# A gated mix of a long convolution and a shift MLP: permuted frequencies, re-homed scratch, and the gate on ScalarE

## The chip, the core and the metric

One core of a Trainium2 chip runs the whole kernel. The metric is device time in microseconds (us) for one execution; a run's time is that of the core from launch to end, and the comparisons use the median of several runs. The engines are TensorE (PE; PEld is its weight load), VectorE (DVE), ScalarE (ACT), GpSimd (POOL) and SyncE (SP), which here only issues DMAs.

## The reference

Two branches share the input x = q of shape (1, 2048, 640), in bf16, and a gate per row mixes them:

```python
x = A_q
g = _sigmoid((x * gate_w).sum(-1, keepdims=True))
a = _A_ref(x, A_k, A_v, A_shift_k, A_ssm_k, A_ssm_D)
b = _B_ref(x, B_w1, B_w2, B_w3, B_w4)
return g * a + (1 - g) * b
```

Branch A: a causal convolution of four taps over k gives k_shift, kv = k_shift * v, then a causal convolution of kv over all 2048 rows with a filter of 2048 taps per channel (`ssm_k`), computed with FFTs of 4096 points along the rows; a skip term kv * ssm_D is added and the result is multiplied by q.

Branch B: h = gelu(layernorm(x) @ w1); the four quarters of its columns are shifted by +1, -1, +2 and -2 rows and multiplied by w2 (x1 = x + hs); then x1 + gelu(layernorm(x1) @ w3) @ w4, with 1536 columns between w3 and w4.

## The kernel before, in words

**Tiles.** Row 16p + n of the sequence lies on partition p in tile n, so there are 16 tiles u = 0 to 15 of 128 x 640, in four groups of four. `Q` holds x and is overwritten with x1 and then with the MLP's result. The hidden rows lie transposed in `GS`, with the row shift made while they are written.

**The long convolution** is a two-step Fourier transform made of matmuls. `step1` multiplies a group of rows by the matrix F1 (128 x 128, cosine and sine part), ACT copies the result from PSUM to an `AR` tile, and ACT's queue stores it to a DRAM scratch tensor: `SH` for the filter (`filt`, 32 units over four groups), `SX` for kv (`signal`, 32 units). `spectrum` runs over 32 groups of frequencies t: `spec_h` reads SH back (BH), multiplies by M2[t] and copies to HS, two DMAs swap the halves of HS; `spec_x` does the same for SX (BX, XPB) and DVE multiplies the two spectra; `spec_z` multiplies by G1[t] and G2[t], copies to ZG (ACT and DVE in turn) and stores to `SZ`. `y_group` reads SZ (ZT), multiplies by F1T, applies the gate and q (`ty`) and adds the other branch.

**The matrices** M2, G1 and G2 are 128 x 4096 each and are made on the chip. POOL writes index patterns, DVE makes integer phases from them (the tile GEN), and ACT takes the sine. A matrix column belongs to one of four residues j, and only the partitions of the same residue may be nonzero: `gen_matrix` therefore runs four sines for each matrix, one for each j, with a scale and a bias for each partition that are zero on the others. Such a masked sine writes 1024 elements:

```python
for j in range(4):
    nc.scalar.activation(out=dst[:, :, :, :, j], in_=jv, func=ACT.Sin,
                         bias=mbias[:, j:j + 1], scale=mscale[:, j:j + 1])
```

**The filter** `A_ssm_k` is loaded as five tiles HN; `filter_transpose` transposes each on PE into the four tiles HT, with ACT and DVE copying from PSUM in turn.

**Branch B** is `norm_stats` and `norm_apply` (DVE statistics, the power for 1/sqrt on POOL, DVE's xn, transposes on PE, DVE's copy to XNT), `first_product` (W1, gelu on ACT into GS), `second_product` (W2, added to Q by DVE), `third_product` (W3, gelu on ACT into G) and `fourth_product` (W4, added to Q by DVE, then scaled by 1 - g on ACT; for the last group on DVE, with the store).

**Gate.** `gate_dot` multiplies x by the gate's weights on POOL and sums on ACT, a tile at a time (scr); `gate_act` makes G32 (g) and OMG (1 - g).

**Short convolution.** `short_conv` needs the taps CJ, laid out from CJR by four POOL copies, the tiles KT and VT of the group, and three rows of the neighbouring partition (KHALO). DVE makes it in acc and tmp.

**Order.** The program is written for one scheduler that keeps, on each engine, the program's order as a priority: an instruction whose inputs and buffers are expected earlier may be put ahead, and the resulting order is fixed for each engine. Waits are for data and for buffers. `merge(a, b, ratio)` interleaves two generators by costs written by hand; a falls first, b gets ratio times its cost. The main sequence is: norms and products for groups 0 and 1 with the filter's transposes, the sine matrices, the gate's first half, then `merge(chain(second_product(US[0]), first_product(2, X2)), filt(), 0.5)`, group 3 and the gate's second half, then the mixer (`mixer_front`) merged with `signal`, then `spectrum` merged with the rest of the MLP, then the output.

**Buffers.** Tiles of one tag share a number of buffers: "b5" has 11 (HN, HT, CJR, CJ, KHALO, KT, VT, acc, tmp, AR, BH, BX, HS, ZG, ZT), "w" has 3 (W12, GEN, W3, W4, XPB), "xnt" 2 (XNT), "g" 3 (the gelu tiles G), "r" 6 (xn, scr, ty, DROW), "gs" 1 (GS, later XQ, a second copy of q). In PSUM the tag "pc" has two (transforms and filter transposes) and "pm" two (the MLP).

Of the kernel before, what the change touches and what calls it, by code (L numbers as in the profile page):

```python
# [9 lines left out]
ACT = mybir.ActivationFunctionType  # L10
# [7 lines left out]
def kernel(  # L18
# [25 lines left out]
    nc = tc.nc  # L44
# [106 lines left out]
    pf4 = consts.tile([P, 1], F32, name="pf4")  # L151
    nc.vector.tensor_scalar(out=pf4[:], in0=pidx[:], scalar1=4.0, scalar2=1.0, op0=ALU.mult, op1=ALU.add)

    GEN = main.tile([P, 15, 256], F32, name="GEN", tag="w", bufs=3)

    def gen_i(a, n, dtype):
        return GEN[:, a:a + n, :].rearrange("p a b -> p (a b)").bitcast(dtype)

# [3 lines left out]
    for gi, (dst, col_mul, col_add, prow) in enumerate(((F1, 4, 1, pf), (F1T, 1, 0, pf4))):  # L162
        ic = gen_i(2 * gi, 1, I32)[:, 0:P]
        nc.gpsimd.iota(ic, pattern=[[col_mul, P]], base=col_add, channel_multiplier=0)
        jj = gen_i(2 * gi + 1, 1, I32).rearrange("p (c k) -> p c k", c=2)
# [9 lines left out]
    M2 = consts.tile([P, KH, 2, 16, 4], BF16, name="M2")  # L175
    G1 = consts.tile([P, KH, 2, 16, 4], BF16, name="G1")
    G2 = consts.tile([P, KH, 2, 16, 4], BF16, name="G2")
    midp = pbits(120, 0.125, 0, "midp")
    klo = pbits(3, 1, 0, "klo")
    basep = pbits(3, 16, 1, "basep")  # L180
    basei = pbits(60, 128, 0, "basei")
    nc.vector.tensor_tensor(out=basei[:], in0=basei[:], in1=basep[:], op=ALU.add)
    offp = [pbits(4, -512, 6144 + 2048 * ro, f"offp{ro}") for ro in range(2)]
    offi = [pbits(64, -64, 6144 - 2048 * o, f"offi{o}") for o in range(2)]
    mscale = consts.tile([P, 4], F32, name="mscale")
    mbias = consts.tile([P, 4], F32, name="mbias")
    for j in range(4):
        nc.vector.tensor_scalar(out=mscale[:, j:j + 1], in0=klo[:], scalar1=float(j), scalar2=2 * PI_ / TU,
                                op0=ALU.is_equal, op1=ALU.mult)
        nc.vector.tensor_scalar(out=mbias[:, j:j + 1], in0=klo[:], scalar1=float(j), scalar2=-PI_,  # L190
                                op0=ALU.is_equal, op1=ALU.mult)
    m0, m1 = gen_i(4, 2, F32), gen_i(6, 2, F32)

    def gen_phase():
        icf, ick, icn = gen_i(8, 2, I32), gen_i(10, 2, I32), gen_i(12, 2, I32)
        nc.gpsimd.iota(icf.rearrange("p (g i n) -> p g i n", i=4, n=16), pattern=[[64, 8], [4, 4], [512, 16]],
                       base=0, channel_multiplier=0)
        nc.gpsimd.iota(ick.rearrange("p (g i n) -> p g i n", i=4, n=16), pattern=[[64, 8], [4, 4], [0, 16]],
# [3 lines left out]
        nc.vector.tensor_scalar(out=m0, in0=icf, scalar1=basep[:], scalar2=midp[:], op0=ALU.add, op1=ALU.mult)  # L202
        nc.vector.scalar_tensor_tensor(out=m1, in0=ick, scalar=basei[:], in1=icn, op0=ALU.add, op1=ALU.mult)

    def gen_matrix(k):
        dst, src, offs = ((M2, m0, (offp[0][:], offp[1][:])), (G1, m1, (offi[0][:], offi[1][:])),
                          (G2, m1, (0.0, 6144.0)))[k]
        slot = (8, 0, 8)[k]
        jj = gen_i(slot, 4, I32)
        for o in range(2):  # L210
            nc.vector.tensor_scalar(out=jj[:, 512 * o:512 * o + 512], in0=src, scalar1=offs[o], scalar2=None,
                                    op0=ALU.add)
        nc.vector.tensor_scalar(out=jj, in0=jj, scalar1=TU - 1, scalar2=None, op0=ALU.bitwise_and)
        jv = jj.rearrange("p (o m n) -> p m o n", o=2, n=16)
        for j in range(4):
            nc.scalar.activation(out=dst[:, :, :, :, j], in_=jv, func=ACT.Sin,  # L216
                                 bias=mbias[:, j:j + 1], scale=mscale[:, j:j + 1])
# [4 lines left out]
    SZ = dram.tile([P, 32, D], BF16, name="SZ")  # L222
# [24 lines left out]
    def filter_transpose(dt):  # L247
        if not HT:
            HT.extend(big("HT") for _ in range(NG))
# [105 lines left out]
    KT, VT = [], []  # L355

    def load_cj():
        cjr = big("CJR", [P, D, 4])
        nc.gpsimd.dma_start(out=cjr[:], in_=A_shift_k.partition_broadcast(P))
        cj = big("CJ")  # L360
        for j in range(4):
# [346 lines left out]
```

## Time and profile before

| | us |
|---|---|
| median of 3 runs (lowest, highest) | 349.83 (349.45, 350.97) |
| profiled execution | 351.51 |
| its span, first to last instruction | 349.7 |
| PE busy | 260.7 |
| DVE busy | 205.3 |
| ACT busy | 193.3 |
| POOL busy | 57.9 |

The DMAs move 59.6 MB, at a mean of 170 GB/s over the span. The mean granted TensorE clock is 0.891 of full speed.

A group's line in the profile reads: source line, engine, operation, output tile <- input tiles, their shapes, count | busy us in all, mean ns of one | us that the engine was idle just before them, and what ended most of it. A line of waits reads: engine, tile and line that waited <- what ended the wait: us in all, times, longest. A windows line gives each engine's busy time and instructions in a stretch of the span, the granted clock, DMA's busy share and GB/s. Matmul durations overlap, so sums of busy time over a stretch are used rather than means. "SPq" and "ACTq" are the queues from which DMAs are issued.

### The profile page before, as it was taken

To read this page: it belongs to the slowest core of one execution; us is meant where nothing else is said; L and a number is where in the kernel's file an instruction comes from. 1 tells how busy PE (TensorE), PEld (TensorE's weight loads), DVE (VectorE), ACT (ScalarE), POOL (GpSimd) and SP (SyncE) were. 2 spreads that over 40 slices of the span, in tenths; PEclk is the share of its full clock that TensorE was granted. 3 is DMA by queue.
4 is the path that set the end of the run, shared out by engine and by line. 5 is a ranking of instruction groups with operands and counts; after the bars stand their busy time and mean duration, and the time that the engine had idled before them with its cause. 6 is when DMAs were issued, how large, how long until landed. Compare 5 with 4: busy or idle time off the path is not lost.

```text
span 349.7 us, 4290 instructions
## 1 busy us (share of the span) xinstructions
PE 260.7 (75%) x1572; PEld 154.7 (44%) x1572; DVE 205.3 (59%) x391; ACT 193.3 (55%) x271; POOL 57.9 (17%) x84
## 2 busy tenths in 40 slices
PE   2445967205683289999999999999999999742685
PEld 1433454002331246457754667446665556421343
DVE  4999956200006985549699993225664444541995
ACT  1123899998899102461456417968766788530000
POOL 4366873119004011100020010000000000000000
PEclk9999989755855559999999999999999999995989
DMA  8999200006669200006222286547897776738943
GB/s 281 245 330 378 81 1 2 0 12 220 219 194 379 103 2 0 3 28 199 75 75 78 75 320 255 147 191 216 237 287 259 221 244 186 225 114 306 366 154 112
DMA packets 32643, 59.59 MB, mean 170 GB/s; under 512 B 7375, under 2 KB 23887, under 8 KB 32622
## 3 DMA queue, kind: packets, MB, share of 16 engines
q1 hardware_dynamic: 19726, 42.77, 38.0%
q10 hardware_dynamic: 12672, 15.73, 12.7%
q0 software_dynamic: 224, 0.82, 0.7%
q8 instruction: 12, 0.20, 0.2%
q14 instruction: 9, 0.07, 0.1%
HBM read 35.71 MB, written 18.35 MB: 155 GB/s over the span
## 4 chain that ended last, share of the span: by engine, by line
PE 44%; DVE 19%; ACT 18%; DMA 11%; SPq 4%; issue 4%; POOL 0%; DVEq 0%; ACTq 0%; POOLq 0%
PE psw L431 11%; PE psw L418 10%; PE psw L321 5%; ACT G L216 5%; PE psz L494 4%; PE psw L404 4%; DMA BX<-SX 4%; DVE xn L279 3%; ACT AR L90 3%; ACT M L216 3%; SPq L124 3%; DVE acc L393 3%; PE ps L233 2%; DVE tmp L391 2%; PE psh L465 2%
## 5 line engine op out<-in xcount | busy, mean ns | idle before, releaser
L431 PE MATMUL psw<-W,G 128*128 128x320 bf16 x384 | 62.2, 303 | 0.1
L418 PE MATMUL psw<-XNT,W 128*128 128x512 bf16 x240 | 57.5, 379 | 0.6 <-DVE XNT L95 0.4
L90 ACT CAST AR<-ps 128x640 bf16<-128x640 f32 x64 | 41.1, 695 | 22.1 <-PE ps L233 22.1
L483 DVE TENSOR_TENSOR XPB<-XPB,HS 128x640 bf16<-128x640 bf16 x64 | 28.5, 487 | 41.1 <-ACT XPB L90 41.1
L431 PEld LDWEIGHTS <-G 128*128 128x128 bf16 x384 | 37.9, 99 | 16.0 <-issue 0.3
L233 PE MATMUL ps<-HT,F 128*128 128x320 bf16 x64 | 19.0, 409 | 22.6 <-ACT HT L90 15.9
L311 ACT ACTIVATE G<-psw 128x1024 bf16<-128x1024 f32 x24 | 24.7, 1029 | 18.6 <-PE psw L418 18.4
L418 PEld LDWEIGHTS <-W 128*128 128x128 bf16 x240 | 23.4, 98 | 24.8 <-issue 1.3
L286 PE MATMUL pst<-IDB,xn 128*128 128x128 bf16 x160 | 16.1, 274 | 23.5 <-DVE xn L279 19.6
L321 PE MATMUL psw<-XNT,W 128*128 128x512 bf16 x100 | 28.2, 439 | 4.9 <-DVE Q L407 2.4
L233 PEld LDWEIGHTS <-F 128*128 128x128 bf16 x128 | 13.6, 108 | 40.5 <-issue 33.9
L265 DVE BATCH_NORM_STATS2 st<-Q 128x6 f32<-128x320 bf16 x64 | 27.3, 466 | 4.1 <-DMA Q<-in_A_q_dram 4.0
L345 POOL TENSOR_TENSOR scr<-Q,GWB 128x640 bf16<-128x640 bf16 x16 | 22.9, 1461 | 36.7 <-ACT scr L346 35.7
L92 ACT ACTIVATE HS<-psh 128x640 bf16<-128x640 f32 x32 | 22.4, 708 | 11.1 <-PE psh L465 10.8
L90 ACT CAST XPB<-psx 128x640 bf16<-128x640 f32 x32 | 22.2, 693 | 6.4 <-PE psx L478 5.9
L494 PE MATMUL psz<-XPB,G 128*128 128x320 bf16 x128 | 22.7, 298 | 3.7 <-DVE ZG L95 1.2
L286 PEld LDWEIGHTS <-xn 128*128 128x128 bf16 x160 | 13.8, 126 | 26.1 <-DVE xn L279 21.2
L404 PE MATMUL psw<-W,GS 128*128 128x320 bf16 x160 | 23.1, 301 | 0.6 <-DVE XNT L95 0.6
L536 PE MATMUL psy<-ZT,F1T 128*128 128x320 bf16 x64 | 13.4, 344 | 13.5 <-DMA ZT<-SZ 8.7
L279 DVE TENSOR_SCALAR xn<-Q,mv,rs 128x640 bf16<-128x640 bf16 x32 | 19.0, 649 | 2.5 <-POOL rs L270 2.5
L539 DVE SCALAR_TENSOR_TENSOR ty<-psy,G,XQ 128x640 bf16<-128x640 f32 x16 | 13.5, 880 | 11.0 <-PE psy L536 11.0
L321 PEld LDWEIGHTS <-W 128*128 128x128 bf16 x100 | 11.1, 111 | 19.9 <-issue 11.4
(97 smaller groups left out, 369.8 us busy)
## 6 DMA issues: line engine op xcount, KB each, us to landing
SH<-AR ACTq DMA_DIRECT2D x8, 640.0 KB, 4.1
SX<-AR ACTq DMA_DIRECT2D x8, 640.0 KB, 3.3
BH<-SH SPq DMA_DIRECT2D x8, 640.0 KB, 4.3
HS<-HS SPq DMA_DIRECT2D x32, 160.0 KB, 3.1
BX<-SX SPq DMA_DIRECT2D x8, 640.0 KB, 4.8
SZ<-ZG ACTq DMA_DIRECT2D x8, 640.0 KB, 3.8
ZT<-SZ SPq DMA_DIRECT2D x8, 640.0 KB, 6.0
W<-in_B_w_dram SPq DMA_DIRECT2D x2, 1920.0 KB, 11.6
```

Of the source, the lines that this page charges most:

```text
L90: nc.scalar.copy(out=o, in_=i)
L216: nc.scalar.activation(out=dst[:, :, :, :, j], in_=jv, func=ACT.Sin, bias=mbias[:, j:j + 1], scale=mscale[:, j:j + 1])
L233: nc.tensor.matmul(ps[:, comp, 0:HD], lhsT=F1[:, comp, :], rhs=src[:, c0:c0 + HD], start=True, stop=True)
L265: nc.vector.bn_stats(out=st[:, h, :], in_=src[i][:, h * HD:(h + 1) * HD])
L279: nc.vector.tensor_scalar(out=xn[:], in0=src[i], scalar1=mv[:, i, 0:1], scalar2=rs[:, i:i + 1], op0=ALU.subtract, op1=ALU.mult)
L286: nc.tensor.transpose(out=pst[:, dd, i * P:(i + 1) * P], in_=xns[i][:, (d0 + dd) * P:(d0 + dd + 1) * P], identity=IDB[:])
L321: nc.tensor.matmul(ps[:, j, :], lhsT=W1P[:, dt, nt * P:(nt + 1) * P], rhs=XNT[:, dt, :], start=(dt == 0), stop=(dt == DT - 1))
L404: nc.tensor.matmul(ps[:, h, 0:HD], lhsT=GS[:, nt, u, :], rhs=W2P[:, nt, h * HD:(h + 1) * HD], start=(nt == 0), stop=(nt == DT - 1))
L418: nc.tensor.matmul(ps[:, j, :], lhsT=W3[:, dt, (f + j) * P:(f + j + 1) * P], rhs=XNT[:, dt, :], start=(dt == 0), stop=(dt == DT - 1))
L431: nc.tensor.matmul(ps[:, h, 0:HD], lhsT=G[ft // 4][:, ft % 4, i * P:(i + 1) * P], rhs=W4[:, ft, h * HD:(h + 1) * HD], start=(ft == 0), sto ...
L483: nc.vector.tensor_tensor(out=xp[:, 1 + a, :], in0=xp[:, 0, :], in1=HS[t // 2][:, a, t % 2, :], op=ALU.mult)
L494: nc.tensor.matmul(pz[:, h, 0:HD], lhsT=gm[:, t].rearrange("p a b c -> p (a b c)"), rhs=XP[t][:, 1 + a, h * HD:(h + 1) * HD], start=(a == ...
```

## The change

- **Layout of the matrices.** The frequencies are permuted so that in M2, G1 and G2 the residue j is no longer the innermost index: M2 is [128, 32, 2, 4, 16] and G1, G2 are [128, 32, 4, 2, 16]. A masked sine then writes runs of 16 (M2) or 32 (G1, G2) neighbouring elements. The inverse's index constants follow, with a mask of their own, and some more constants of one column are made.
- **SZ** is [4, 32, 32, 640]; a ZG tile is stored with one step over all 128 partitions. Each row is still a run of 1280 bytes, each ZT read four rows in a run.
- **Phases.** The 15 KB tile GEN in "w" gives way to three tiles of 4 KB in "g". `gen_phase` and the three `gen_matrix` become `gen_forward` (M2), placed ahead of the first norm, and `gen_inverse` (G1, G2), placed ahead of the first product.
- **HT.** Three of its four tiles become one tile HTA in "w"; the fourth, HTB, stays in "b5".
- **CJR** moves to "xnt", and `load_cj` to the start of the sequence. The halo and the first KT, VT are written ahead of the first product, the second KT, VT ahead of the filter's transform.
- **Sequence.** The filter's transform is merged with `second_product(US[0])` alone; X2's norm, `first_product(2)` and the statistics of group 3 come behind it, with the first two parts of `signal`'s short convolution between them. The gate's first half comes ahead of the filter's last transpose, its second half behind `first_product(2)`. `mixer_front` is merged with the rest of `signal` at 0.6.
- **Spectrum.** The four XQ loads stand within it, at t = 10, 14, 18 and 22. The last `third_product` is taken out of the merge, whose ratio becomes 0.75, and runs behind it.
- **End.** `ty` is made in two steps: ACT copies from PSUM with the scale g, DVE multiplies by XQ in bf16.

```diff
-    GEN = main.tile([P, 15, 256], F32, name="GEN", tag="w", bufs=3)
+    def gen_tile():
+        t = main.tile([P, 1024], I32, name="GEN", tag="g", bufs=3)
+        return t[:]
+
+    GA, GB, GC = gen_tile(), gen_tile(), gen_tile()
...
-    M2 = consts.tile([P, KH, 2, 16, 4], BF16, name="M2")
-    G1 = consts.tile([P, KH, 2, 16, 4], BF16, name="G1")
-    G2 = consts.tile([P, KH, 2, 16, 4], BF16, name="G2")
+    M2 = consts.tile([P, KH, 2, 4, 16], BF16, name="M2")
+    G1 = consts.tile([P, KH, 4, 2, 16], BF16, name="G1")
+    G2 = consts.tile([P, KH, 4, 2, 16], BF16, name="G2")
...
+    def masked_sines(dst, jj, ms, inner):
+        nc.vector.tensor_scalar(out=jj, in0=jj, scalar1=TU - 1, scalar2=None, op0=ALU.bitwise_and)
+        jv = jj.rearrange("p (o m n) -> p m o n", o=2, n=16)
+        for j in range(4):
+            nc.scalar.activation(out=dst[:, :, :, j, :] if inner else dst[:, :, j, :, :], in_=jv, func=ACT.Sin,
+                                 bias=ms[:, 1, j:j + 1], scale=ms[:, 0, j:j + 1])
+
+    def gen_forward():
+        icf = GA[:, 0:512]
         nc.gpsimd.iota(icf.rearrange("p (g i n) -> p g i n", i=4, n=16), pattern=[[64, 8], [4, 4], [512, 16]],
                        base=0, channel_multiplier=0)
+        for ro in range(2):
+            nc.vector.tensor_scalar(out=GC[:, 512 * ro:512 * ro + 512], in0=icf, scalar1=midp[:],
+                                    scalar2=offp[ro][:], op0=ALU.mult, op1=ALU.add)
+        masked_sines(M2, GC, masks[0], True)
+
+    def gen_inverse():
+        ick, icn, m1 = GA[:, 512:1024], GB[:, 0:512], GB[:, 512:1024].bitcast(F32)
...
         nc.vector.scalar_tensor_tensor(out=m1, in0=ick, scalar=basei[:], in1=icn, op0=ALU.add, op1=ALU.mult)
+        for (dst, jj, offs) in ((G1, GA, (offi[0][:], offi[1][:])), (G2, GC, (0.0, 6144.0))):
+            for o in range(2):
+                nc.vector.tensor_scalar(out=jj[:, 512 * o:512 * o + 512], in0=m1, scalar1=offs[o], scalar2=None,
+                                        op0=ALU.add)
+            masked_sines(dst, jj, masks[1], False)
...
-    SZ = dram.tile([P, 32, D], BF16, name="SZ")
+    SZ = dram.tile([4, 32, 32, D], BF16, name="SZ")
...
-            HT.extend(big("HT") for _ in range(NG))
+            hta = weights("HTA", [P, 3, 4, D])
+            HT.extend([hta[:, g] for g in range(3)] + [big("HTB")[:]])
...
-        cjr = big("CJR", [P, D, 4])
+        cjr = main.tile([P, D, 4], BF16, name="CJR", tag="xnt", bufs=2)
...
-                tensor=SZ.tensor, offset=SZ[16 * kg, 0, 0].offset,
-                ap=[[D, 32], [128 * D, 4], [32 * D, 4], [1, D]]), in_=zg[:])
+                tensor=SZ.tensor, offset=SZ[0, 4 * kg, 0, 0].offset,
+                ap=[[D, P], [1024 * D, 4], [1, D]]), in_=zg[:])
...
+            if t % 4 == 2 and 2 <= t // 4 < 6:
+                g = (3, 0, 1, 2)[t // 4 - 2]
+                nc.sync.dma_start(out=XQ[:, 4 * g:4 * g + 4, :], in_=qv[:, 4 * g:4 * g + 4, :])
...
-            nc.vector.scalar_tensor_tensor(out=halves(ty[:]), in0=ps[:, :, 0:HD], scalar=G32[:, u:u + 1],
-                                           in1=halves(XQ[:, u, :]), op0=ALU.mult, op1=ALU.mult)
+            evac("a", halves(ty[:]), ps[:, :, 0:HD], G32[:, u:u + 1])
+            nc.vector.tensor_tensor(out=ty[:], in0=ty[:], in1=XQ[:, u, :], op=ALU.mult)
...
+    CJ = load_cj()
+    gen_forward()
     st0 = norm_stats(tiles_of(c4[0]))
...
     filter_transpose(1)
-    gen_phase()
+    gen_inverse()
...
     load_q(3)
+    KHALO = load_halo()
+    load_kv(0)
     X1 = norm_apply(tiles_of(c4[1]), st1, "v")
     run(first_product(0, X0))
-    st2 = norm_stats(tiles_of(c4[2]))
     filter_transpose(2)
     filter_transpose(3)
     run(first_product(1, X1))
-    gen_matrix(0)
-    gen_matrix(1)
-    gen_matrix(2)
+    st2 = norm_stats(tiles_of(c4[2]))
     gate_dot(0)
-    X2 = norm_apply(tiles_of(c4[2]), st2, "v")
+    gate_dot(1)
     filter_transpose(4)
-    gate_dot(1)
-    KHALO = load_halo()
-    CJ = load_cj()
-    load_kv(0)
     W3 = weights("W3", [P, DT, Fh])
     nc.sync.dma_start(out=W3[:], in_=B_w3.rearrange("(kt p) f -> p kt f", p=P))
-    merge(chain(second_product(US[0]), first_product(2, X2)), filt(), 0.5)
+    load_kv(1)
+    sig = signal()
+    merge(second_product(US[0]), filt(), 1.0)
+    X2 = norm_apply(tiles_of(c4[2]), st2, "v")
+    next(sig)
     st3 = norm_stats(tiles_of(c4[3]))
+    run(first_product(2, X2))
+    next(sig)
     sy0 = norm_stats(tiles_of(US[0]))
+    gate_dot(2)
+    gate_dot(3)
     W4 = weights("W4", [P, FT, D])
     nc.sync.dma_start(out=W4[:], in_=B_w4.rearrange("(kt p) e -> p kt e", p=P))
-    gate_dot(2)
-    gate_dot(3)
...
-    merge(mixer_front(), signal(), 0.65)
+    merge(mixer_front(), sig, 0.6)
     XPB = weights("XPB", [P, 4, 3, D])
     XQ = main.tile([P, N2, D], BF16, name="XQ", tag="gs")
-    for g in (3, 0, 1, 2):
-        nc.sync.dma_start(out=XQ[:, 4 * g:4 * g + 4, :], in_=qv[:, 4 * g:4 * g + 4, :])
-    merge(spectrum(), chain(third_product(Ys[0], G_[2]), fourth_product(US[2], G_[2], False),
-                            third_product(Ys[1], G_[3])), 1.0)
+    third3 = third_product(Ys[1], G_[3])
+    merge(spectrum(), chain(third_product(Ys[0], G_[2]), fourth_product(US[2], G_[2], False)), 0.75)
+    run(third3)
```

## The prediction

> **What bounds the kernel now.** I read the page's busy slices first, then cut the span into stages with the windows view, then the groups and the waits of the stages that looked loose. In the slices each digit is a fortieth of the span, 8.7 us:
>
> ```profile
> PE   2445967205683289999999999999999999742685
> ACT  1123899998899102461456417968766788530000
> PEclk9999989755855559999999999999999999995989
> DMA  8999200006669200006222286547897776738943
> ```
>
> From slice 15 (134 us) on PE is full, so that part is bounded by TensorE. Before it PE is not full, ACT is (slices 5 to 12), DMA is nearly at rest for slices 5 to 8, and the granted TensorE clock falls to half. The stages, cut at 32 (first product begins), 50, 79 (the filter's first transform matmul), 108.5 (its last), 134 (mixer begins), 221.5 (spectrum), 312.5 (its last store), 321.7 (its result is back):
>
> ```profile
> core 0: us, PE busy (x) PEld busy (x) DVE busy (x) ACT busy (x) POOL busy (x), PEclk, DMA share, GB/s
> 0.00:32.00 32.00, 11.87 (x103) 10.77 (x104) 26.02 (x79) 7.59 (x12) 16.50 (x36) 1.00 0.96 300
> 32.00:50.00 18.00, 15.40 (x90) 8.30 (x89) 14.27 (x40) 14.30 (x22) 13.26 (x19) 0.96 0.27 106
> 50.00:79.00 29.00, 10.29 (x60) 5.83 (x58) 9.91 (x22) 28.99 (x19) 8.37 (x8) 0.74 0.04 7
> 79.00:108.50 29.50, 21.55 (x72) 8.62 (x71) 1.56 (x2) 25.47 (x43) 7.61 (x8) 0.62 0.68 234
> 108.50:134.00 25.50, 12.47 (x68) 7.30 (x69) 19.89 (x25) 8.52 (x24) 6.82 (x8) 0.57 0.30 109
> 134.00:218.00 84.00, 81.16 (x538) 50.53 (x537) 65.49 (x102) 38.79 (x54) 5.34 (x6) 1.00 0.32 113
> 221.50:312.50 91.00, 84.27 (x511) 49.22 (x509) 43.17 (x84) 67.07 (x98) 0.00 (x0) 1.00 0.71 217
> 312.50:321.70 9.20, 1.25 (x4) 0.59 (x5) 0.00 (x0) 0.00 (x0) 0.00 (x0) 0.62 0.69 247
> 321.70:346.70 25.00, 19.31 (x108) 11.48 (x107) 22.66 (x36) 0.00 (x0) 0.00 (x0) 0.87 0.66 245
> ```
>
> Between 50 and 79 ACT is busy for all 29 us and PE for a third; ACT was busy for only 7.6 of the first 32. What fills it, by form (count, sum, mean ns):
>
> ```profile
> L311 ACT ACTIVATE G<-psw 128x1024 bf16<-128x1024 f32 x24 | 24.7, 1029 | 18.6 <-PE psw L418 18.4
> L216 ACT ACTIVATE G<-GEN,mbias,mscale 128x1024 bf16<-128x1024 int32 x8 | 19.1, 2603 | 0.0
> L216 ACT ACTIVATE M<-GEN,mbias,mscale 128x1024 bf16<-128x1024 int32 x4 | 10.2, 2673 | 0.0
> L170 ACT ACTIVATE F<-GEN,NPI 128x256 bf16<-128x256 int32 x1 | 0.5, 508 | 8.0 <-DVE GEN L169 8.0
> ```
>
> The twelve masked sines cost 29.3 us, 2.5 times a gelu of as many elements. The waits name what stands behind them, what blocks DVE next, and what opens the end:
>
> ```profile
> PE ps L233 <- ACT HT L90: 15.9, 1, 15.9
> DVE acc L390 <- DMA SH<-AR: 28.4, 1, 28.4
> PE psy L536 <- DMA ZT<-SZ: 8.7, 2, 8.4
> ```
>
> The filter's step1 (L233) waits for the last HT copy, queued on ACT behind the sines. Then DVE stands 28.4 us at the short convolution's first product, whose buffer an AR tile of the filter holds, and the norms X3 and Y0 stand behind that product on DVE. Last, PE waits 8.4 us for the spectrum to come back from DRAM.
>
> **The sum's base.** The profiled execution took 351.5 us, its span 349.7, so 1.8 lie around the span; the median of the runs is 349.83, 1.7 lower. I work in differences on the profiled execution and take them from the median. A difference under 0.5% is about what a measurement here can't tell from none.
>
> **Sines.** After the change each writes runs of 16 (M2) or 32 (G1, G2) neighbouring bf16; now it writes every fourth. No row shows a 1024-element sine written in runs. Lowest: the gelu, 1.03. Highest: as now, 2.67. The nearest row is F: sine, int32 in, contiguous out, 0.508 for 256. Two gelus of 512 and 1024 elements take 602 and 1029 ns, 0.83 ns an element; 768 more on F make 1.15 us, which I take because operation and input type are the same: 12 x 1.15 = 13.8 instead of 29.3, 15.5 saved. The reads keep their runs of 16 int32, as now.
>
> The Trainium skill's "ScalarE: Activation LUTs" (What ACT_TABLE_LOAD costs) says that every function runs at one element a cycle, which makes an estimated 1.23 us with two pointer operands; the 2.6 us rows don't keep it. A rule against the change stands in "SBUF — State Buffer" (Door 1): two accesses to a 16-byte line give full bandwidth. A step of 8 bytes has two to a line, so by that rule the stores are already at full rate, the sines stay at 2.6 us, and the sum is the first rival's. F against M and G speaks for the store; no run shows it yet.
>
> **Their place.** M2 goes ahead of all norms, G1 and G2 ahead of the first product. The first 32 us have 24.4 us of idle ACT, so 13.8 fit. What may spoil it: DVE, which makes the phases (some 7 us of work before and after, plus some 17 tiny constants at 0.065, 1.1 us), is busy 26 of 32. That work was nearly all before 40 us already. If G1 and G2 (9.2 us) slip behind 32, they meet an ACT that is busy 14.3 of 18, of which one M sine (2.75) and three table loads (1.28 each) go: 10.3 are free. The cover holds, and without it some 5 us are lost. A Sin after a Gelu reloads the table; with all sines ahead, two or more of five loads go.
>
> So the filter's first matmul moves from 79 to about 50: 79 less the 29.3 of sines, and again: PE is done with first product 1 at about 46 (32.4 and two times 7.0, below), then 16 transposes (2 us), two HT copies (0.6 each) and the row addition (0.5). Gain 29.
>
> **Early loads.** CJR is loaded first on POOL's queue (640 KB, landing 9.0 before) and its four copies (2.8) stand ahead of the powers for rs on POOL. X0 may be up to 5 us late; the first product begins only at 32 because X1's xn took 5.6 instead of 0.42 while POOL's gate products ran, so X0 has 15 us to spare. I take 0, keeping -4 to +4. KT0, VT0 and the halo are issued on SP where they were, and KT1 and VT1 ahead of W4, which waits anyway for a slot.
>
> **Filter.** 32 evacuations; two took 1.47 us where TensorE was at half clock (.735 each), so 23.5 instead of 29.5, as first product 2 with its gelus and table load is taken out of between. It ends at about 73.5.
>
> **To the mixer.** First product 2 costs 7.0 on PE (28.2 for four). Beside it DVE has two parts of the convolution (5.1), statistics (8 x 0.466 + 4 x 0.197 = 4.5), xn (1.7), XNT (1.6), and PE's transposes 1.5: X3 is ready at 88. First product 3 takes 7.0, its gelus and Y0 another 3: the mixer begins at 98 instead of 134. Bounds: everything of DVE done earlier, 73.5 + 14 = 88; both products at half clock (10.7 each) and all of DVE's two norms (20.6) in line, 108. Gain 36, from 26 to 46. ACT has room for it: from 50 to 98 it has 23.5 of AR, 6.4 of two products' gelus and 13 gate sums of 0.92 that were not before 36, 42 of 48; POOL has 13 x 1.46 = 19. These gate products change their place in the program, not their number. SBUF allows it too: three of four HT tiles leave the pool of 11 big buffers, so 4 are left for AR where 3 were.
>
> **Mixer.** PE 81.2 of 84 busy: it moves as it is. DVE has 65.5 and loses 5. I take 0.
>
> **Spectrum and end.** PE is the bound (84.3 of 91). Third product 3 (60 of 240 matmuls that take 57.5: 14.4) and the half of the last fourth product that ran there (48 of its 96 matmuls come after 321.7, 30 of them in 4.26, so 7) move behind it; 63 of PE are left, ACT has 67.1 less six gelus, 60.9. DMA: 0.71 x 91 = 64.6, plus the four XQ loads, 640 KB at 376 GB/s 1.75 each, 71.6. At the 0.9 that DMA reached at its fullest slices that is 79: gain 12. Third product 3 (14.4) fills the 9.2 us of the way through DRAM: +5. At the end DVE has per tile 0.49 + 0.49 instead of 0.88 + 0.49, and ACT, which is at rest there, 0.71 to 0.83: two tiles took 2.39 and take 1.8, 4 us over 6.5 pairs; half a fourth product more on PE (7) takes most of it, as PE then has a floor of 23 (96 x 0.142 and 64 psy matmuls x 0.145) against 25 now: -1. Together -8, between -15 (third product 3 also fills holes of the spectrum) and +5 (XQ loads delay BX). SZ's stores and loads keep 1280 and 5120 bytes a run: 0.
>
> Sum: -36 - 8 = -44, 349.8 - 44 = 306. The bounds together, -61 to -21, give 289 to 329.
>
> **Rivals.**
> 1. The sines stay at 2.6 us. For: no such row. Against: F. Then G1 and G2 take 20.8 from about 24, first product 0's gelus wait from 34.5 to 45, the filter starts at 60: gain 26 + 8, 316.
> 2. Spectrum bound by reads. For: DMA at 0.8 and a BX wait of 7.5 us on the chain. Against: BH is read two groups ahead. If each XQ load (7.1 to landing) delays a BX by as much, +28: 334.
> 3. Slower: AR starves. KT1, VT1 now live through the filter; with CJ, the halo, KT0, VT0 and HTB 7 of 11 are held, with acc and tmp 9. If AR is left with one, each of its 8 stores is waited for: 2.9 of evacuation and 4.1 to 6.2 of landing, 56 to 73 instead of 23.5. It decides from +44, all of the gain: with +49, 355. Against: the slots go in order of the program, AR before acc, and two already take away most of the price.
>
> **Chances.** Forecast 0.76, the rivals 0.10, 0.07 and 0.07. Of the third 0.02 lands within 0.5%: faster 0.93, same 0.02, slower 0.05. The range of 290 to 331 holds the first rival, and leaves out the second and the third (0.14) and 0.06 of far ends of the forecast.
>
> **What would show it.** Sine group near 1.15 us; the filter's first matmul near 50 and its last near 74; no 28 us wait of DVE for AR; mixer at 98; a spectrum of some 79 us, then third product 3 in place of the wait for ZT; gate evacuations on ACT near 0.75. Wrong: sines at 2.6, or AR's stores on the chain.

## The result, and the profile after

The kernel after takes 326.27 us (median of 4 runs, 325.4 to 328.12) where the kernel before took 350.0 in the same session: a ratio of 0.9326, with an interval of 0.9278 to 0.9374. The prediction said 306, with a range of 290 to 331. Direction and range held; 20 of the 44 us that I expected to gain did not come. The profiled execution took 325.4 us, its span 323.6. Every ratio in this document leaves out runs that were over 1.5% longer than the fastest of their kernel, at a lower granted clock: two of run 4's four and one of run 10's.

The page's busy slices of the kernel after, a fortieth of the span each, now 8.1 us:

```profile
PE   2254796887306999999999999999999999634775
ACT  1265997689800326443563368586779776521750
PEclk9999999999955899999999999999999999975899
DMA  7999900248940002422112975577896776439763
```

The plateau of PE begins at slice 13 (105 us) instead of 15 (131 us). A hole is left ahead of it: in slice 11 (89 to 97 us) PE and ACT do hardly anything (0.6 and 0.4 of the 8 us). The stages cut where the prediction's landmarks came to lie, with the columns of the windows view as before: filter's first transform matmul 52.5, its last 81, mixer 110.4, spectrum 195.9, its last store 287.8, its result back 296.4.

```profile
core 0: us, PE busy (x) PEld busy (x) DVE busy (x) ACT busy (x) POOL busy (x), PEclk, DMA share, GB/s
...
52.50:81.00 28.50, 21.10 (x128) 11.73 (x129) 13.31 (x25) 22.72 (x42) 12.35 (x10) 1.00 0.45 146
81.00:110.40 29.40, 13.83 (x73) 7.95 (x75) 17.36 (x24) 8.73 (x21) 5.11 (x10) 0.71 0.42 150
110.40:195.90 85.50, 83.05 (x558) 52.20 (x561) 68.40 (x105) 41.62 (x59) 5.67 (x6) 1.00 0.33 116
195.90:287.80 91.90, 85.00 (x511) 49.76 (x515) 43.54 (x85) 66.24 (x98) 0.00 (x0) 1.00 0.69 215
287.80:296.40 8.60, 1.25 (x4) 0.57 (x5) 0.00 (x0) 0.00 (x0) 0.00 (x0) 0.50 0.71 260
296.40:320.60 24.20, 19.05 (x108) 11.04 (x107) 17.49 (x36) 11.94 (x16) 0.00 (x0) 0.89 0.72 254
```

Against the landmarks of before and those predicted (us):

| | before | predicted | after |
|---|---|---|---|
| a masked sine | 2.60 to 2.67 | 1.15 | 1.23 |
| first product starts | 32.4 | 32.4 | 35.4 |
| filter, first and last transform matmul | 79, 108.5 | 50, 73.5 | 52.6, 80.9 |
| mixer starts | 133.9 | 98 | 110.4 |
| spectrum, start to last store | 91.0 | 79 | 91.9 |
| way through DRAM that PE waits out | 9.2 | filled | 8.6 |
| last stage | 25.0 | 24 | 24.2 |

One unit of the filter's 32 ran at 50.05 us in the kernel before, too; 79 is the start of the other 31. Between the two profiles, whose spans differ by 26.1 us, 23.5 lie ahead of the mixer and 2.1 in it; the spectrum and the end, from which I expected 8, give half a microsecond. The sines and the gate's evacuation, by form on ACT:

```profile
L92 ACT ACTIVATE ty<-psy,G 128x640 bf16<-128x640 f32 x16 | 11.9, 790 | 16.1 <-PE psy L552 15.6 <-ACT ty L92 0.5
L205 ACT ACTIVATE G<-GEN,msi 128x1024 bf16<-128x1024 int32 x8 | 9.2, 1228 | 2.4 <-DVE GEN L202 2.4
L205 ACT ACTIVATE M<-GEN,msf 128x1024 bf16<-128x1024 int32 x4 | 4.6, 1231 | 0.2 <-DVE GEN L202 0.2
```

And the waits that replaced those of before (engine, tile and line <- what ended the wait: us in all, times, longest):

```profile
PE pst L298 <- DVE xn L291: 18.8, 6, 10.6
DVE acc L402 <- DMA SH<-AR: 11.1, 1, 11.1
PE psy L552 <- DMA ZT<-SZ: 9.4, 3, 7.8
DVE tmp L402 <- ACT scr L358: 7.9, 1, 7.9
```

The wait of 28.4 us for an AR buffer is not gone, it is shorter: 11.1 us for `acc`, ending at 77.6, then 7.9 for `tmp`, ending at 87.1. The row of `tmp` names ACT's gate sum, but `tmp` doesn't use it; the trace's semaphores show a wait for the filter's sixth store, which landed at 86.9. That store and the two behind it took 10.2 to 11.2 us to land, the five ahead of them 3.1. They share the DMAs (share 1.00 from 76 to 88.5 us) with the 1.9 MB of W4, and the change itself sends that load there: W4 now takes the slot of HTA and is issued at 76.03, when PE has read HTA for the last time.

```profile
SPq L660 <- PE ps L244: 18.6, 1, 18.6
```

Some 7 us of the wait for `tmp` are thus the late store's; no run takes W4's load away. Four parts of the short convolution follow on DVE, and X3's xn stands behind them: it comes at 95.9, and PE waits 10.6 us for it.

### The profile page after: what moved, and what is told of

Same layout as the page of the kernel before. It is cut to its first block, busy times and chain, and to the rows that moved or that the text cites. A ratio compares the mean times of both kernels' runs of the same rounds, so it can differ in the third digit from the quotient of the medians.

```text
span 323.6 us, 4307 instructions
## 1 busy us (share of the span) xinstructions
PE 251.2 (78%) x1559; PEld 151.1 (47%) x1572; DVE 201.2 (62%) x406; ACT 183.3 (57%) x283; POOL 56.9 (18%) x84
## 4 chain that ended last, share of the span: by engine, by line
PE 39%; DVE 34%; ACT 12%; DMA 11%; issue 3%; SPq 1%; POOL 0%; ACTq 0%; POOLq 0%; DVEq 0%
PE psw L443 12%; PE psw L430 6%; DVE st L277 5%; PE psw L333 5%; DVE acc L405 5%; PE psz L506 5%; DVE xn L291 4%; DVE tmp L403 4%; DVE Q L419 4%; DMA BX<-SX 4%; ACT AR L90 3%; DMA ZT<-SZ 3%; DVE XNT L95 3%; PE psy L552 2%; PE ps L244 2%
## 5 line engine op out<-in xcount | busy, mean ns | idle before, releaser
L443 PE MATMUL psw<-W,G 128*128 128x320 bf16 x384 | 61.0, 299 | 0.9 <-ACT G L323 0.5
L430 PE MATMUL psw<-XNT,W 128*128 128x512 bf16 x231 | 56.2, 379 | 0.8 <-DVE XNT L95 0.4
L495 DVE TENSOR_TENSOR XPB<-XPB,HS 128x640 bf16<-128x640 bf16 x64 | 28.5, 487 | 32.5 <-ACT XPB L90 32.5
L333 PE MATMUL psw<-XNT,W 128*128 128x512 bf16 x96 | 25.6, 417 | 6.5 <-DVE XNT L95 4.0
L416 PE MATMUL psw<-W,GS 128*128 128x320 bf16 x160 | 24.0, 299 | 2.4 <-DVE Q L419 2.0
L298 PEld LDWEIGHTS <-xn 128*128 128x128 bf16 x160 | 13.0, 118 | 24.7 <-DVE xn L291 21.5
L95 DVE CAST ZG<-psz 128x640 bf16<-128x640 f32 x16 | 13.2, 822 | 12.9 <-PE psz L506 12.9
L92 ACT ACTIVATE ty<-psy,G 128x640 bf16<-128x640 f32 x16 | 11.9, 790 | 16.1 <-PE psy L552 15.6
L333 PEld LDWEIGHTS <-W 128*128 128x128 bf16 x100 | 10.7, 107 | 20.0 <-issue 11.6
L416 PEld LDWEIGHTS <-GS 128*128 128x128 bf16 x160 | 15.5, 98 | 9.5 <-issue 3.2
```

The lines of the kernel that those rows point to most:

```text
L92: nc.scalar.activation(out=o, in_=i, func=ACT.Copy, scale=scale)
L298: nc.tensor.transpose(out=pst[:, dd, i * P:(i + 1) * P], in_=xns[i][:, (d0 + dd) * P:(d0 + dd + 1) * P], identity=IDB[:])
L333: nc.tensor.matmul(ps[:, j, :], lhsT=W1P[:, dt, nt * P:(nt + 1) * P], rhs=XNT[:, dt, :], start=(dt == 0), stop=(dt == DT - 1))
L416: nc.tensor.matmul(ps[:, h, 0:HD], lhsT=GS[:, nt, u, :], rhs=W2P[:, nt, h * HD:(h + 1) * HD], start=(nt == 0), stop=(nt == DT - 1))
L430: nc.tensor.matmul(ps[:, j, :], lhsT=W3[:, dt, (f + j) * P:(f + j + 1) * P], rhs=XNT[:, dt, :], start=(dt == 0), stop=(dt == DT - 1))
L443: nc.tensor.matmul(ps[:, h, 0:HD], lhsT=G[ft // 4][:, ft % 4, i * P:(i + 1) * P], rhs=W4[:, ft, h * HD:(h + 1) * HD], start=(ft == 0), sto ...
```

## The experiments

Several kernels use `tc.issue_after(i)`, which queues what it encloses behind instruction i on the engine of i and adds no wait for its end. "Ratio" is always against the kernel before on the same chip; the kernel after stands at 0.9326.

**1. The layout alone, on the kernel before** (its frequencies then come out in another order).

```diff
-    M2 = consts.tile([P, KH, 2, 16, 4], BF16, name="M2")      # and G1, G2
+    M2 = consts.tile([P, KH, 2, 4, 16], BF16, name="M2")
-            nc.scalar.activation(out=dst[:, :, :, :, j], in_=jv
+            nc.scalar.activation(out=dst[:, :, :, j, :], in_=jv
```

> The kernel before, with nothing changed but the layout in which the masked sines write (runs of 16); the index constants stay, so the frequencies come out in another order than the rest expects. Theory (the store's step makes a sine 2.6 us, and ACT is the path from 41 to 77): the twelve sines fall to about 1.2 us, 14.7 in all instead of 29.3, and the filter's transform starts some 14 us earlier: 336. Rival (the place of the sines in the program matters, not their length; PE or DVE end the stage anyway): 347 or more. Second rival (the reads or the int32 input make them slow): sines stay at 2.6 us, 350.

333.88 us, ratio 0.9533 (0.9478 to 0.9589).

**2. All of the change but the layout:** M2, G1 and G2 as [.., 2, 16, 4] again.

```diff
-            nc.scalar.activation(out=dst[:, :, :, j, :] if inner else dst[:, :, j, :, :], in_=jv
+            nc.scalar.activation(out=dst[:, :, :, :, j], in_=jv
```

> The changed kernel with the masked sines written at a step of four elements again, in the changed order (frequencies out of order). Theory: sines at 2.6 us; G1's and G2's eight end at about 50 instead of 38, the first gelu stands behind them, +12: 338. Rival (in the new place they lie in ACT's idle time whatever their length): 328 or less.

337.73 us, ratio 0.9649 (0.9585 to 0.9713). The group of G in the first run and in the second, by form:

```profile
L216 ACT ACTIVATE G<-GEN,mbias,mscale 128x1024 bf16<-128x1024 int32 x8 | 9.1, 1229 | 0.0
```

```profile
L205 ACT ACTIVATE G<-GEN,msi 128x1024 bf16<-128x1024 int32 x8 | 19.2, 2618 | 2.0 <-DVE GEN L202 2.0
```

The store's step makes the 1.39 us a sine, in either order of the program; the two edits agree with each other and with the two kernels. By the ratios, of 350 us, the layout alone brings 16.3 us, everything else alone 12.3, both 23.6: they overlap by 5.0, which would fit an order that hides part of slow sines.

**3. The gate's evacuation back on DVE.**

```diff
-            evac("a", halves(ty[:]), ps[:, :, 0:HD], G32[:, u:u + 1])
-            nc.vector.tensor_tensor(out=ty[:], in0=ty[:], in1=XQ[:, u, :], op=ALU.mult)
+            nc.vector.scalar_tensor_tensor(out=halves(ty[:]), in0=ps[:, :, 0:HD], scalar=G32[:, u:u + 1],
+                                           in1=halves(XQ[:, u, :]), op0=ALU.mult, op1=ALU.mult)
```

> The changed kernel with ty made by one DVE instruction from PSUM again, as before. Theory (the end is PE's floor of some 23 us, ACT's copies gave 1 us of the 24.2): 327. Rival one (ACT's part was worth the 4 us worked out for DVE): 330. Rival two (ACT adds a hop to each tile and costs): 325 or less.

326.02 us, ratio 0.9319 (0.9278 to 0.936): this part of the change is worth nothing that can be measured.

**4. The convolution out of X3's way.** The two `next(sig)` between the norms go, and the first four of group 0's five parts are held behind the last norm's copy on DVE.

```diff
+    with tc.issue_after(LASTV[0].ins):        # DVE's last copy to XNT
+        for _ in range(4):
+            next(sig)
     gate_act()
     run(first_product(3, X3))
```

> The changed kernel with the first four parts of the short convolution put behind X3's and Y0's copies on DVE. Theory (X3's norm waits on DVE behind convolution parts that wait for AR's buffers): X3's xn come once the gate sums free their rows, at about 88, the mixer starts at 103 instead of 110: 319. Rival (the convolution is only moved, and the mixer then waits for kv): 326, with the same time between the filter's end and the spectrum's start.

The median is 321.65 us; the ratio of 0.9078 (0.899 to 0.9166) rests on two runs of 316.5 and 319.0 us. Their granted clock was 0.978 and 0.976, while that of the kernel after was 0.945 to 0.958. At 0.950 and 0.958 this kernel took 324.3 and 324.8, some 2 us less than the kernel after, so the ratio can't be set beside the others. The profile, taken at 0.958, shows first product 3 starting at 93.7 instead of 103.1 and the mixer at 101.75 instead of 110.4, so X3 did wait for the convolution.

**5. The gate's second half behind the norms as well**, written ahead of that hold.

> As f1_conv_behind, and the second half of the gate's products also behind X3 and Y0, so that their row buffers don't hold back xn. Theory: X3 is ready before first product 2 ends, the third follows it, the mixer starts at about 95: 312. Rival one (the mixer is then short of kv or gates and gives it back): 322 or more. Rival two (row buffers don't matter): as f1.

323.05 us, ratio 0.9228 (0.9175 to 0.928). First product 3 starts at 88.1, but PE now waits 3.4 us in it, because the gate's sums stand ahead of its gelu on ACT, and the mixer begins at 101.5, no sooner than in run 4. Of the 8.9 us gained there, 6.1 come back by the spectrum's start (193.1 instead of 195.9): the mixer now holds 75.3 us of DVE's work in 91.6, where it was 68.4 in 85.5.

**6. The first group early.** Group 0 and its product with V are written ahead of the filter's transform, `load_kv(1)` behind it; group 1 is held as group 0 was in run 4, and the gate's second half stands behind the norms.

```diff
-    load_kv(1)
     sig = signal()
+    for _ in range(5):
+        next(sig)
     merge(second_product(US[0]), filt(), 1.0)
+    load_kv(1)
```

> The changed kernel with the short convolution of group 0 written ahead of the filter's transform, so that acc and tmp get their buffers before AR, KT1 and VT1 loaded behind it, the parts of group 1 held behind X3's and Y0's copies on DVE, and the gate's second half behind these norms. Theory (DVE stood 19 us for AR's buffers with X3 behind it, and with the convolution behind X3 the mixer has too little DVE left, 91 us instead of 85.5): DVE does group 0 in its idle time at 43 to 49, no wait for AR stands ahead of X3, the mixer starts near 98 and keeps its 85 us: 314. Rival one (AR, with fewer buffers, waits for its stores: the filter ends 5 to 10 us later): 322 or more. Rival two (what X3 gains the mixer gives back, being bound by DVE or PE): 321 to 323, as in f1 and f2.

319.45 us, ratio 0.9127 (0.9092 to 0.9162): 6.8 us better than the kernel after. DVE does the group between 38.8 and 54.7 (it had been idle for 5.9 us between 35.4 and 52.5), and no AR tile stands between it and X3. The filter ends 5 us later, at 85.8; first product 3 starts at 93.9. But the eight sums of the gate, each waiting for POOL's product, hold its gelus on ACT from 90.5 to 102.6, and the mixer begins at 113.2, later than the 110.4 of the kernel after. So the gain isn't ahead of the mixer: from the mixer's start to the spectrum's last store it is 169.1 us instead of 177.4. Group 1 of the convolution, too, is nearly done when the mixer begins, which leaves 58.3 us of DVE's work in its 82.1; that this is the cause is my reading and has no run of its own.

**7. The gate last:** run 6, with the gate's second half behind first product 3, its products held behind the copies to GS on POOL and its sums behind the gelus on ACT.

> The kernel after, with the first group of the short convolution ahead of the filter's transform (as in the run before this one), and the gate's second half behind first product 3: its products on POOL are held behind that product's copies to GS, its sums on ACT behind that product's gelus. Theory: the second half of the gate was the last thing ahead of first product 3, which was held from 100 to 108.9 by sums queued ahead of its gelus on ACT; the mixer starts at 102 instead of 113.2. About half of that is given back, since the sums and three groups of the convolution now lie in the mixer beside an ACT that is half busy: 319.45 - 5 = 314. Rival: all of it is given back, because the mixer's DVE work (60 to 65 us of 85 there) sets its pace: 319. Second rival: POOL's products beside DVE hold DVE back in the mixer: 322.

324.29 us, ratio 0.9278 (0.923 to 0.9326), slower than all three had it, and nearest to the second rival, whose mechanism it shows. First product 3 did go at once, and the second product began at 97.7. Then PE stood, in the waits between 50 and 115 us:

```profile
PE psw L427 <- DVE Q L430: 10.1, 1, 10.1
```

The second product's two PSUM tiles were full, and DVE's addition that empties them stood behind group 1 of the convolution, which was stretched: an addition of 2560 elements took 2.56 us beside POOL's gate products (2.1 each) where it had taken 1.49 in run 6 once those were done. Group 1 itself had waited 3.5 us for an AR store. What runs 4 to 7 have in common is that each took something from ahead of X3 and put it ahead of, or beside, the next thing that PE needs.

**8. Two groups early, the rest behind what it had held.** Groups 0 and 1 ahead of the filter's transform; the gate as in run 7; `second_product(US[1])` on its own, and all of the signal's rest held behind its last addition on DVE and behind the gelus on ACT.

```diff
     sig = signal()                            # now groups 2, 3 and all of step1
+    load_kv(1)
+    run(short_conv(0), short_conv(1))
     merge(second_product(US[0]), filt(), 1.0)
...
+    run(second_product(US[1]))                # taken out of mixer_front
-    merge(mixer_front(), sig, 0.6)
+    merge(mixer_front(), held(sig, LASTQ[0].ins, LASTG[0].ins), 0.6)
```

> The kernel after with the order of its middle written anew: the short convolution's groups 0 and 1 ahead of the filter's transform, in the time in which DVE is idle (13.7 us between 74 and 87.7 in the run before this one, and more between 37 and 66); the gate's second half behind first product 3's copies on POOL and its gelus on ACT; second_product(US[1]) on its own, ahead of the rest of the signal, whose parts are held behind its last addition on DVE and behind those gelus on ACT. Theory: nothing of another branch then stands ahead of X3, of first product 3 or of the additions of US[1]; the filter ends at 86, X3 goes at once, the second product runs from 98 to 103 without the 10.1 us wait for DVE's additions, and the mixer, with 25 us of convolution where the kernel after has some 37, is PE's 81 us: spectrum at 184 instead of 195.9, total 326.3 - 12 = 314. Rival: what is taken away comes back in the mixer as before, because the transform's evacuations and the gate's sums (14.5 + 7.6 us) crowd the gelus on ACT there: 320, as with the first group alone. Second rival: the second group delays X2's norm by its 12 us, so first product 2 and with it X3: mixer at 108, 322.

317.47 us, ratio 0.9093 (0.9014 to 0.9172). The second rival's mechanism is there (X2's norm waits for the second group, the filter ends at 92.5 and the mixer begins at 104.7), but nothing comes back: from the mixer's start to the spectrum's last store it is 175.2 us, in the kernel after 177.4.

**9. The last third product behind the spectrum.** In the kernel after it was written behind the merge, but the scheduler put its matmuls into it again (some at 240 to 265 us), as it put the XQ loads ahead of it (all four at 178.0 to 179.5). Here it is held on PE behind the last psz matmul.

```diff
-    run(third3)
+    with tc.issue_after(LAST[0].ins):         # PE's last psz matmul
+        run(third3)
```

> The changed kernel with the last third product held behind the spectrum's last psz matmul on PE's queue. In the changed kernel it ran inside the spectrum (its matmuls at 240 to 265 of the profile), and PE waited 7.8 us for ZT with nothing to do. Theory (the step of the prediction that failed: the merge's order doesn't hold it back, so PE had the same work in the spectrum as before): the spectrum falls from 92 us to 79 to 82, the third product fills the wait for ZT (14.4 in place of 8.6): total -4 to -7, 320 to 322. Rival (the spectrum's own chain through two PSUM buffers and the DMAs is what takes 92 us): the spectrum stays near 90 and the third product adds 6: 332.

326.59 us, ratio 0.9332 (0.9288 to 0.9376): no change. The third product filled the way through DRAM, but the spectrum, with 13 us less for PE, still took 90:

```profile
195.40:285.50 90.10, 71.81 (x414) 40.59 (x415) 44.74 (x86) 61.27 (x92) 0.00 (x0) 0.96 0.70 219
```

No engine and no DMA is full in this row. One t takes 2.5 us while PE is nearly full (210 to 241 us, by ZG's copies) and still 2.4 afterwards, so something other than PE's work sets the pace.

**10. Is it the PSUM buffers?** Three tiles a t (psh, psx, psz) share two buffers; psz goes to the MLP's two.

```diff
-        pz = ps_tile("psz", "pc")
+        pz = ps_tile("psz", "pm")
```

> The kernel after with one edit: spec_z's PSUM tile comes from the MLP's two buffers (tag pm) and not from the two of the transforms (tag pc). Theory: the spectrum's pace of 2.35 us for one t is a chain through two PSUM buffers: three tiles a t, of .43 + .70, .43 + .69 and .70 + .69 us for matmul and evacuation, 3.64 in all or 1.82 a t over two buffers, and some 0.1 to 0.2 for each of three handovers. With the third tile elsewhere ACT is next, 1.4 for HS and XPB, half of 0.69 for ZG and a little for the filler's gelus, about 2.0 a t: 32 x 0.35 is 11 at most, and where the third product shares the buffers (half of the stage) half of that is lost: 326.3 - 7 = 319, spectrum of 84 us instead of 91.9. Rival: reads of BX and the DMAs (share 0.68 to 0.76 there) are as late, so no change: 326. Second rival: third and fourth product wait for the buffers that psz holds, slower: 330.

327.65 us, ratio 0.935 (0.9293 to 0.9408): no gain. (With psz there, the scheduler leaves the last third product behind the spectrum by itself.) But the waits of this stage changed. In the kernel after, 196 to 288 us, and in this one, 196 to 290:

```profile
PE psx L490 <- DMA BX<-SX: 1.7, 2, 1.4
...
PE psh L477 <- DMA BH<-SH: 0.6, 1, 0.6
```

```profile
PE psx L490 <- DMA BX<-SX: 8.2, 3, 3.3
PE psh L477 <- DMA BH<-SH: 4.3, 1, 4.3
```

Now the reads are late. A read lands 5 to 6 us after its issue, in time if issued when written; but it stands on SP's queue behind the swaps of HS, and those wait for ACT. On that queue in the kernel after:

```profile
SPq L482 <- ACT HS L92: 63.8, 16, 15.7
```

So whether the PSUM buffers bound the stage at all is open: this run shows no gain from them.

**11. The same, with BH and BX read from POOL's queue**, which is at rest in the spectrum.

```diff
-        nc.sync.dma_start(out=t[:].rearrange("p i d -> p (i d)"), in_=bass.AP(
+        nc.gpsimd.dma_start(out=t[:].rearrange("p i d -> p (i d)"), in_=bass.AP(
```

> The kernel after with two edits in the spectrum: spec_z's PSUM tile from tag pm, as in the run before, and the reads BH and BX issued from POOL's queue (POOL is at rest there) instead of SP's, where each stands behind the swaps of HS, which wait for ACT (63.8 us in all on SP). Theory: with the PSUM chain gone the waits for BX went from 1.7 to 8.2 us and for BH from 0.6 to 4.3, since the reads are issued late; issued on their own they come in time, ACT's 2.0 us a t is the bound, spectrum of 84 us instead of 91.9: 319. Rival: the buffers that the reads need come free as late as the swaps do, so the queue changes nothing: 326. Second rival: issuing from POOL takes longer to land than 5 to 6 us: 330.

318.51 us, ratio 0.9082 (0.9035 to 0.9129): 7.8 us better than the kernel after, as the theory had it. The spectrum of run 10 and of this one, with the same work in it:

```profile
195.70:287.60 91.90, 71.73 (x413) 40.94 (x412) 44.67 (x86) 60.92 (x93) 0.00 (x0) 0.93 0.68 215
```

```profile
196.00:277.80 81.80, 68.38 (x408) 39.90 (x412) 44.86 (x86) 60.51 (x93) 7.42 (x14) 0.96 0.75 233
277.80:287.00 9.20, 9.20 (x43) 4.19 (x43) 0.00 (x0) 3.89 (x4) 0.00 (x0) 1.00 0.54 180
```

A read lands later from POOL (6.9 us in the median for BX, 5.8 from SP in run 10), and it doesn't matter, since its issue no longer stands behind the swaps. PE's idle time before psx falls from run 10's 8.2 us for BX to

```profile
  DMA BX<-SX: 1.3, 1
```

The row from 277.8 is the third product in the place of the wait for ZT. Whether the queue alone would do, with psz left where it was, wasn't tried.

**12. Runs 8 and 11 together.**

> The two edits that paid, together: the middle of the order written anew with two groups of the short convolution early, and in the spectrum psz from tag pm with BH and BX read from POOL's queue. Theory: they act on stages that follow each other, so the gains add: 326.3 - 8.8 - 7.8 = 309.7, with the last third product in the place of the wait for ZT. Rival: with the first edit alone PE was already busy for 94 of 96 us of the spectrum, so the pace of its chain no longer counts there and only the 6 us wait for ZT is to be had: 312 to 314. Second rival: POOL's gate products and its reads, or the spectrum's early start beside the mixer's end, put the reads behind POOL's work: 318.

312.08 us (309.68 to 314.14 in 6 runs), ratio 0.8917 (0.8876 to 0.8957): the fastest version, 14.2 us below the kernel after. The granted clock of its runs spread from 0.955 to 0.977; the three at 0.955 to 0.961 took 312.8 to 314.1, so some of the 14.2 may be the clock's. The sum would have been 309.7, and the rival's 312 to 314 is nearer. The spans say why: 309.6 against 315.3 for run 8, and run 8's wait was

```profile
PE psy L564 <- DMA ZT<-SZ: 7.6, 3, 6.1
```

In run 8 PE was already busy for 94.0 of the 96 us from 184 to 280, so the pace of the chain counted there no more:

```profile
184.00:280.00 96.00, 94.00 (x597) 57.47 (x602) 49.44 (x94) 68.68 (x100) 1.24 (x2) 1.00 0.65 215
```

The wait of 6.1 us is what the second edit takes, and it is filled by a third product which had been part of those 94.

## Why the prediction was right or wrong

**What held.** The first bound (ACT's sines ahead of the filter) and the cure (runs instead of steps) are shown by runs 1 and 2. The twelve took 13.8 us of busy time (9.2 and 4.6), as the sum had it, and that is partly luck: a sine came to 1.23 us instead of 1.15, but neighbours overlap by some 0.09 (eight in a row, 9.83 us by their mean, are busy for 9.17), which the sum left out. The estimate of 1.23 from "ScalarE: Activation LUTs" (What ACT_TABLE_LOAD costs) was the better one, 1.228 to 1.231 here, and the 2.6 shows that it doesn't hold for stores in steps of 8 bytes. The rule of "SBUF — State Buffer" (Door 1) that I weighed against the change doesn't hold for these stores: by it a step of 8 bytes is at full rate, and runs 1 and 2 measure 1.23 against 2.62 with only the step changed. The first rival fell with it. The mixer moved as it was, 85.5 us against 87.6 (its DVE work did not fall by the 5 I named: 67.9 us before, 68.4 after), and the last stage gave 0.8 of the predicted 1, for which run 3 shows the gate's evacuation not to be needed.

**The start.** "I take 0, keeping -4 to +4": it came to +3. DVE is busy 29.9 of the first 35.4 us, where it was 26.0 of 32, and the filter's start, 52.6, is late by 2.6. That DVE's added work is the reason is likely; no run takes it out.

**The filter's length, 23.5 predicted, 28.3 measured.** The 32 evacuations were cheaper than I took them (19.9 us, not 23.5). I had counted the gate's sums against ACT's room between 50 and 98 (13 of them, where the trace of before has 15 after 36 us), but not in this line, where four of them lie (3.8 with their accumulator reads), and I had ACT never waiting: it was idle for 5.8 of the 28.5, 2.6 of it behind DVE's copy of HTA and 3.1 behind PE, which was at X2's transposes and first product 2. The term was short by 4.8.

**From the filter to the mixer, 24.5 predicted, 29.5 measured.** This is the step that failed. I put "two parts of the convolution (5.1)" beside first product 2 and asked only what they cost, not what they wait for. Their buffers, `acc` and `tmp`, come after AR in the order of the slots, so DVE waits 11.1 and 7.9 us for the filter's stores, and X3 behind it. I had also written that W4 "waits anyway for a slot", and not asked what the load would meet when the slot came free: it met the last three of these stores. That is the third rival's mechanism (AR tiles scarce) at the place where I had seen it in the kernel before, and I had priced it only where AR itself waits. Runs 4 to 6 show it: with the convolution behind X3 or ahead of AR, first product 3 starts at 93.7, 88.1 and 93.9 instead of 103.1. Runs 5 to 7 show that the time can't be had by moving one piece, since ACT's gate sums and then DVE's additions stand next in line.

**The spectrum, 79 predicted, 91.9 measured.** Two errors. I took the place in the source for the place in time: third product 3 and the XQ loads stayed where they had been. And I took a stage with PE at 84 of 91 for one that PE bounds, and 63 us of PE with DMA at 0.9 for its price without the filler. Run 9 took the filler out and the stage kept its length, so PE was not the only bound. Run 11 against run 10 shows another, the reads queued behind the swaps (91.9 us to 81.8). That the chain through two PSUM buffers was a third is argued, not shown: moving psz alone gained nothing, and the queue without it wasn't tried. With both edits the stage took 81.8 us and the way through DRAM was filled; that this is close to my 79 is luck, since that figure was DMA at 0.9 and the share was 0.75. The second rival (reads bound the spectrum) had the right resource at the wrong cause: not XQ in front of BX, but HS.

**The bounds.** The gain ahead of the mixer, given as 36 with 26 to 46, came to 23.5, below its low end: the start's 2.6, the filter's 4.8 and the 5.0 behind it have the same sign, since each stage was priced as if its engine alone set its length. The low end was also summed wrongly: 73.5, two products of 10.7 and 20.6 of norms in line make 115.5, not 108, and so a gain of 18.5, which would have held the 23.5. The total stayed in the range, but near its edge: 23.7 us were gained, and the smallest gain that the bounds together allow is 21.

## What to carry to other kernels

When a stall moves away, look at what is queued behind the stalled instruction and what each of those waits for in turn: an edit that takes one from the front usually shows the next, and the gain comes only when the whole queue ahead of the needed instruction is free. Before a transfer's place in the source is counted as an edit, look in the trace at when it is issued, and at what its queue's earlier entries wait for; a queue of transfers that depend on compute is a poor place for a prefetch. When a load waits for a buffer, look at what will be on the DMAs at the time the buffer comes free. A stage with one engine at 93% may have a second bound just below: take the filler out of it once, and see whether it gets shorter.

## What was not expected of the hardware

- ACT's 1024 bf16 results in steps of 8 bytes took 2.62 us, in runs of 16 or 32 elements 1.23, with the same reads.
- DVE's bf16 addition of 2560 elements took 1.49 us with POOL at rest and 2.56 beside POOL's two-input products of 640, which took 2.1 us there and 1.46 in the kernel before.
- The filter's stores of 640 KB took 3.1 us to land, and 10.2 to 11.2 beside a load of 1.9 MB issued just ahead of them.
- The reads that POOL's queue issued held POOL for 0.53 us each and landed later than from SP: BX after 6.9 us in the median instead of 5.2 and 5.8 (kernel after, run 10), BH after 5.6 instead of 4.7 and 5.0.
